# A new list of steps for chunk-selected attention and a gated MLP, planned with one reader at a time on a PSUM bank

## The chip, the cores and the metric

The kernel runs on one core of a Trainium2 chip. The metric is the device time of one execution, in microseconds, as the median of several runs. A profile is taken of one execution.

## The reference

Attention over 4 batches of 8 heads, 768 tokens, 64 columns a head, and then an MLP on the 3072 tokens of 512 columns.

```python
k_min, k_max = min and max of k over chunks of 32 keys
ub = sum(maximum(q * k_min, q * k_max), axis=-1)      # a bound per query and chunk
ub = where(causal, ub, -1e9)
sel = the 6 chunks with the largest ub, of each query
scores = where(sel & causal, q @ k.T / 8, -1e9)
attn = softmax(scores);  x = attn @ v                 # 8 heads side by side
h = x @ w_in                                          # 512 -> 2048
out = (h * clip(h + 3, 0, 6) / 6) @ w_out             # 2048 -> 512
```

## The kernel before

The work is cut into units and groups. A *unit* is half a batch of queries (384 tokens) for four heads, which are two *pairs* of heads; units u0 to u3 are batch 0, u4 to u7 batch 1, and so on, and pairs p0 to p3 are batch 0. In every batch the first two units are half 0, the other two half 1. A *group* is half a batch with all heads: g0 to g7.

For a pair and half the steps are: `turn` (TensorE transposes the keys, KS, or queries, QS, into a PSUM bank in batch 0; VectorE does it in later batches), `turn_out` (the queries' bank is copied to SBUF), `keys` (cast of the keys' bank), `limits` (two reductions on VectorE for minimum and maximum of each chunk, part 0, and a subtraction, part 1), `queries` (a relu, read from the bank in batch 0, and a cast). In batch 0 the keys' bank thus has two readers, `keys` and `limits`, and the queries' bank two, `turn_out` and the relu. Then, for a unit, `bounds` (TensorE), `bounds_in`, `bias`, `largest`, `select`, `guard`, `select_out` (VectorE, with POOL for some): the choice of chunks, which ends in a mask that `masks_out` copies beside the queries in batches 1 to 3. For a pair again: `scores` (TensorE, in two or four tiles), `exponentials` (ScalarE), `triangle` (POOL cuts the diagonal blocks), `values` (TensorE) and `values_out` (VectorE). `beside` and `shifted` copy constant mask rows next to keys.

For a group: `turn_tokens` (TensorE) or, for three groups, `turn_words`, a round trip through DRAM and `part_words`; `hidden` 0 to 15 (TensorE), `hidden_relu` and `hidden_out`; `result` (four parts of four matmuls per tile of 128 tokens, TensorE), `result_scale`, and a store on SP. The names with what they work on, as scores(p0 0 0) or hidden(g0 0), are used below.

K, Q and V are loaded by SP in an order written out in `SEQ` (line 661), four weight loads (two halves of w_in, WIN, and two of w_out, WOUT) are issued by POOL. Each weight load first reads a word of the input load that stands before it, so POOL waits there for that landing.

The order is planned while the program is built. `Plan.add` collects some 1,645 steps with the engines that can do them, what they come after, and which buffers they take and give (`m=4` PSUM banks for mixed use, `s=2` double banks for scores, and others). `Plan.order` (lines 74 to 132) runs through time with estimated lengths: whenever an engine is free it starts the ready step of the lowest rank for which there is room, and the steps are issued to the engines in that sequence. A rank comes from the list `PLACES` (line 978): the number of each listed step, in order. `ONLY` (line 1021) says which of the steps that several engines could do is done by which. Not listed are the loads and stores and 24 dummy matmuls (`busy`, line 339), which have the highest ranks and fill TensorE before the first inputs are there. `LANDED` (line 699) tells the planner when input loads land. On the chip the engines run their queues in the issued order and wait for each other by semaphores.

The readers of a bank in `prepare` (lines 801 to 824) and the list are what the change touches:

```python
turned[name] = seen[name] if name == "KS" else add(dict(ACT=0.45, DVE=0.52), None, r + lead, later(turn_out, st, name, half),
                                                   after=[seen[name]], take=[held[f]], give=[m])
...
for place, i in enumerate(PLACES.split()):
    plan.steps[int(i)]["rank"] = place, int(i)
```

Of the kernel before, what the change touches and what calls it, by code (L numbers as in the profile page):

```python
# [140 lines left out]
def kernel(  # L141
# [523 lines left out]
    plan = Plan(m=4, s=2, kf=4, qf=6, qr=6, ub=3, mt=2, pt=10, x=2, xt=2, bt=2, bd=2, gt=2, u=3, ot=2, vt=3, ks=2, qs=2, sel0=1, sel1=1, lane=8)  # L665
# [6 lines left out]
    def later(f, *args):  # L672
        return lambda *engine: f(*args, *engine)
# [6 lines left out]
    def arrive(engine, issue, length, run, after=(), take=(), parts=1):  # L680
# [3 lines left out]
        for part in range(parts):  # L684
# [14 lines left out]
    LANDED = dict(SP=[7.05, 7.65, 8.27, 8.87, 9.46, 10.07, 10.67, 11.26, 11.87, 12.47, 13.08, 13.68, 14.28, 14.88, 15.48, 16.08, 16.68, 17.28, 17.95, 19.70, 20.10, 20.50, 21.00, 21.40, 21.80, 22.35, 22.95, 23.55, 24.10, 25.10,  # L699
                      26.80, 41.00, 49.90, 51.40, 52.90, 54.20, 55.70, 57.20, 58.60, 60.00, 61.40, 62.80, 64.10, 64.80, 67.20, 68.80, 69.50, 70.40, 71.40, 72.20, 73.00, 73.70],  # L700
                  POOL=[33.30, 38.70, 44.50, 50.40])
# [379 lines left out]
```

## Time and profile before

| | |
|---|---|
| median of 3 runs | 266.26 us (266.20 to 266.56) |
| the profiled execution | 266.23 us |
| its span, first to last instruction | 264.4 us |
| TensorE (PE) busy | 258.8 us, 98% |
| VectorE (DVE) | 211.4 us, 80% |
| ScalarE (ACT) | 193.0 us, 73% |
| GpSimd (POOL) | 122.7 us, 46% |
| granted TensorE clock | full in all of 40 slices |

The span is counted from the first instruction; the execution's time also holds what lies around it. Line numbers (L350) are those of the kernel before. Matmuls are pipelined and their ends are modelled, so a busy TensorE can hide a wait. The chain is followed back from the last instruction: at each step to what released it.

### The profile page before, as it was taken

The page shows a single profiled execution, that of the slowest core. Times are in us where ns is not written, and L with a number is a line of the kernel's source. Part 1 is how long each engine was busy: PE and PEld are TensorE (multiplying, and loading weights), DVE is VectorE, ACT ScalarE, POOL GpSimd, SP SyncE. Part 2 cuts the span into 40 slices and gives each one's busy share as a digit, 9 for nine tenths or more (in the row PEclk, how much of TensorE's full clock was granted, in tenths as well). Part 3 has the DMA queues.
Part 4 walks back from the last instruction along what each step waited for, and adds up shares of the span by engine and source line. Part 5 has one row for each costly group of instructions (what it writes and reads, how often), then busy time and mean ns, then how long its engine had stood idle before and what let it go on. Part 6 is the DMA issues. An engine that isn't in the chain of part 4 may idle for free.

```text
span 264.4 us, 6698 instructions
## 1 busy us (share of the span) xinstructions
PE 258.8 (98%) x2468; PEld 153.8 (58%) x2468; DVE 211.4 (80%) x587; ACT 193.0 (73%) x318; POOL 122.7 (46%) x286
## 2 busy tenths in 40 slices
PE   8999999999999999999999999999999999999995
PEld 4547657655545666655655576654666575645543
DVE  6698987999979899997979799999997056905920
ACT  5869798597866999994986699965988686703601
POOL 8355624265545764465174793776464241020000
PEclk9999999999999999999999999999999999999999
DMA  8999999999949999951981999423000411132012
GB/s 165 219 211 174 209 198 217 167 133 159 233 117 135 145 199 134 138 134 42 151 70 45 216 166 136 99 102 116 26 0 4 159 42 41 62 99 79 2 40 79
DMA packets 121280, 32.15 MB, mean 122 GB/s; under 512 B 113056, under 2 KB 116896, under 8 KB 121248
## 3 DMA queue, kind: packets, MB, share of 16 engines
q1 hardware_dynamic: 116512, 27.14, 61.9%
q0 software_dynamic: 3136, 4.19, 9.3%
q10 hardware_dynamic: 1600, 0.39, 0.7%
q8 instruction: 19, 0.31, 0.5%
q14 instruction: 13, 0.11, 0.2%
HBM read 28.44 MB, written 7.47 MB: 136 GB/s over the span
## 4 chain that ended last, share of the span: by engine, by line
PE 87%; ACT 6%; DVE 2%; DMA 2%; issue 1%; ACTq 1%; DVEq 0%
PE HP L607 30%; PE OP L625 30%; PE SPS L517 10%; PE PVP L550 7%; ACT PT L529 4%; PE UBT L435 4%; DMA QS<-in_q_dram 2%; PE SPS L498 1%; PE OP L634 1%; PE XTP L571 1%; PE SPS L501 1%; ACTq L198 1%; PE SPS L342 1%; DVE KMA L374 1%; DVE KMA L375 1%
## 5 line engine op out<-in xcount | busy, mean ns | idle before, releaser
L529 ACT ACTIVATE PT<-SPS 128x1024 bf16<-128x1024 f32 (+2 forms) x96 | 84.8, 922 | 12.4 <-PE SPS L517 5.7
L607 PE MATMUL HP<-XT,WIN 128*128 128x384 bf16 x512 | 90.0, 326 | 0.0
L625 PE MATMUL OP<-WOUT,GT 128*128 128x512 bf16 x368 | 85.6, 379 | 0.0
L615 ACT ACTIVATE U<-HP,THREE 128x384 bf16<-128x384 f32 x100 | 57.4, 584 | 18.5 <-PE HP L607 14.6
L618 DVE SCALAR_TENSOR_TENSOR GT<-U,HP 128x384 bf16<-128x384 bf16 x128 | 66.2, 544 | 4.7 <-ACT U L615 2.4
L607 PEld LDWEIGHTS <-WIN 128*128 128x128 bf16 x512 | 48.5, 98 | 32.2 <-issue 1.9
L625 PEld LDWEIGHTS <-GT 128*128 128x128 bf16 x368 | 35.0, 98 | 37.2 <-issue 1.1
L534 POOL TENSOR_SCALAR_AFFINE_SELECT PT<-PT 128x256 bf16<-128x256 bf16 x84 | 33.9, 413 | 45.9 <-ACT PT L529 44.8
L517 PE MATMUL SPS<-QLA,KL 128*128 128x384 bf16 (+2 forms) x240 | 35.9, 278 | 0.5 <-ACT PT L529 0.4
L517 PEld LDWEIGHTS <-KL 128*128 128x128 bf16 x240 | 21.6, 98 | 12.9 <-issue 1.5
L651 ACT ACTIVATE OT<-OP 128x512 f32<-128x512 f32 x17 | 10.2, 597 | 24.6 <-PE OP L625 24.1
L550 PEld LDWEIGHTS <-PT 128*128 128x128 bf16 x672 | 24.3, 97 | 4.3 <-DVE Xb L562 0.3
L550 PE MATMUL PVP<-VB,PT 128*128 128x65 bf16 x672 | 25.9, 193 | 0.0
L309 POOL TENSOR_SCALAR_AFFINE_SELECT KL<-KF 64x384 bf16<-64x384 f32 x37 | 18.4, 501 | 8.2 <-DVE KF L359 7.1
L309 POOL TENSOR_SCALAR_AFFINE_SELECT QLA<-QF 64x384 bf16<-64x384 f32 (+1 forms) x32 | 16.0, 502 | 10.6 <-DVE QF L359 3.6
L562 DVE TENSOR_TENSOR Xb<-PVP,RINV 128x384 bf16<-128x384 f32 x32 | 18.2, 570 | 1.1
L613 DVE TENSOR_SCALAR U<-HP 128x384 bf16<-128x384 f32 x28 | 15.3, 547 | 3.5 <-PE HP L607 3.4
L556 DVE RECIPROCAL RINV<-PVP 128x6 f32<-128x6 f32 x32 | 5.9, 185 | 12.3 <-PE PVP L550 12.1
L392 ACT ACTIVATE QR<-QF 128x192 bf16<-128x192 f32 (+2 forms) x36 | 13.2, 413 | 1.7 <-DVE QF L359 1.6
L653 DVE TENSOR_SCALAR OT<-OP 128x512 f32<-128x512 f32 x6 | 4.1, 684 | 12.6 <-PE OP L625 12.6
L374 DVE TENSOR_REDUCE KMA<-KF 128x12 f32<-128x384 f32 x24 | 13.0, 540 | 0.3
L600 POOL COPY XT<-BF 128x384 bf16<-128x384 bf16 x12 | 5.6, 505 | 16.4 <-DMA BF<-BD 16.4
(92 smaller groups left out, 309.3 us busy)
## 6 DMA issues: line engine op xcount, KB each, us to landing
out_dram<-OT SPq DMA_DIRECT2D x23, 256.0 KB, 2.3
KS<-in_k_dram SPq DMA_DIRECT2D x24, 192.0 KB, 5.5
QS<-in_q_dram SPq DMA_DIRECT2D x24, 192.0 KB, 5.8
VT<-in_v_dram SPq DMA_DIRECT2D x24, 192.0 KB, 4.6
WIN<-in_moe_w_in_dram POOLq DMA_DIRECT2D x2, 1024.0 KB, 10.9
WOUT<-in_moe_w_out_dram POOLq DMA_DIRECT2D x2, 1024.0 KB, 19.4
VS<-in_v_dram SPq DMA_DIRECT2D x12, 128.0 KB, 3.7
KS<-in_k_dram SPq DMA_DIRECT2D x9, 128.0 KB, 3.9
```

What stands on the lines that cost most here:

```text
L309: nc.gpsimd.affine_select(out=to, in_=x, pattern=[[0, n]], compare_op=A.is_ge, fill=0.0, base=0, channel_multiplier=0)
L374: nc.vector.tensor_reduce(out=over, in_=chunks, axis=X_AXIS, op=A.max)
L517: nc.tensor.matmul(SP[:, j, c0:c0 + n], lhsT=KLS[st["pair"] % 6][:, j, jb * P:(jb + 1) * P], rhs=st["QL", half][:, j, at:at + n], start=Tr ...
L529: nc.scalar.activation(PT[:, :, 0:cols], SP[:, :, 0:cols], ACT.Exp, scale=scale)
L534: nc.gpsimd.affine_select(out=PT[:, :, c0:c0 + P], in_=PT[:, :, c0:c0 + P], pattern=[[0, 2], [1, P]], compare_op=A.is_ge, fill=0.0, base=0 ...
L550: nc.tensor.matmul(PVP[:, j, n, :], lhsT=PT[:, j, c0:c0 + P], rhs=st["VB"][:, jb, j, :], start=(jb == 0), stop=(jb == qb))
L562: nc.vector.tensor_tensor(out=to, in0=PVP[:, :, :, 0:D], in1=RINV[:].to_broadcast([P, 2, HB, D]), op=A.mult)
L607: nc.tensor.matmul(HP[:], lhsT=WIN[:, kt, f * P:(f + 1) * P], rhs=g["XT"][:, kt, :, :], start=(kt == 0), stop=(kt == KT_HID - 1))
L613: nc.vector.tensor_scalar(U[:], g["HP", f][:], 3.0, 0.0, op0=A.add, op1=A.max)
L615: nc.scalar.activation(U[:], g["HP", f][:], ACT.Relu, bias=THREE[:], scale=1.0)
L618: nc.vector.scalar_tensor_tensor(out=g["GT"][:, f, :], in0=g["U", f][:], scalar=6.0, in1=g["HP", f][:], op0=A.min, op1=A.mult)
L625: nc.tensor.matmul(g["OP", t][:], lhsT=g["GT"][:, f, t * P:(t + 1) * P], rhs=WOUT[:, f, :], start=(f == 0), stop=(f == FT - 1))
```

## The change

Three things change. The planner gets 16 new holds, `r0` to `r15`, one for each turned bank of batch 0 (keys or queries, pair, half), each with room for one; every reader of a bank takes the hold of its bank and gives it back, so the planner lets one engine at a time read it. The planner's landing times are replaced by new ones. And the list has new places for its 1,329 steps: 150 of the steps that several engines can do are given to another engine.

```diff
-    plan = Plan(m=4, s=2, ..., lane=8)
+    plan = Plan(m=4, s=2, ..., lane=8, **{f"r{i}": 1 for i in range(2 * H)})
...
-    LANDED = dict(SP=[7.05, 7.65, 8.27, 8.87, 9.46, 10.07, 10.67, 11.26, 11.87, 12.47, 13.08, 13.68, 14.28, 14.88, 15.48, 16.08, 16.68, 17.28, 17.95, 19.70, 20.10, 20.50, 21.00, 21.40, 21.80, 22.35, 22.95, 23.55, 24.10, 25.10,
-                      26.80, 41.00, 49.90, 51.40, ...],
-                  POOL=[33.30, 38.70, 44.50, 50.40])
+    LANDED = dict(SP=[7.05, 7.65, 8.25, 8.84, 9.45, 10.04, 10.64, 11.24, 11.85, 12.47, 13.06, 13.66, 14.26, 14.86, 15.47, 16.07, 16.66, 17.27, 17.84, 19.43, 19.91, 20.33, 20.72, 21.05, 21.57, 22.10, 23.01, 23.59, 24.07, 25.11,
+                      27.59, 41.46, 50.28, 51.20, ...],
+                  POOL=[32.30, 38.62, 44.06, 49.91])
...
+            def alone(name):
+                return [hold(f"r{4 * p + 2 * half + (name == 'QS')}")] if first else []
...
+                    one = alone(name)
                     turned[name] = seen[name] if name == "KS" else add(dict(ACT=0.45, DVE=0.52), None, r + lead, later(turn_out, st, name, half),
-                                                                       after=[seen[name]], take=[held[f]], give=[m])
+                                                                       after=[seen[name]], take=[held[f]] + one, give=[m] + one)
...
+            one = alone("KS")
             made["K", p, half] = [add(dict(DVE=0.52, ACT=0.51) if first else castings(first), None, r + lead + 1, later(keys, st, half, j), port=not first,
-                                      after=[a] + free.get(("KL", p - 6), []), give=read) for j in range(1 if first else 2)]
-            b1 = add("DVE", 1.0 if first else 0.93, r + lead, later(limits, st, half, 0), after=[a] + free.get(("KM", p - 6), []), give=read)
+                                      after=[a] + free.get(("KL", p - 6), []), take=one, give=read + one) for j in range(1 if first else 2)]
+            one = alone("KS")
+            b1 = add("DVE", 1.0 if first else 0.93, r + lead, later(limits, st, half, 0), after=[a] + free.get(("KM", p - 6), []), take=one, give=read + one)
...
-                             after=[seen["QS"] if first else c], take=[u["qr", p]], give=banks.get("QS", [u["qf", p]]), port=not first)]
+                             after=[seen["QS"] if first else c], take=[u["qr", p]] + one, give=banks.get("QS", [u["qf", p]]) + one, port=not first)]
...
     PLACES = """
-        156 337 153 335 160 144 164 147 146 152 155 157 159 168 331 145 165 161 167 169 158 162 170 163 166 181 154 171 333 172 185 184 182 186 190
...
+        156 154 331 152 335 333 146 159 164 147 153 145 337 144 157 160 155 167 165 158 161 168 170 163 162 169 166 173 181 171 177 172 184 176 178
+        174 185 182 175 183 190 180 231 179 186 191 187 239 188 192 236 189 244 193 232 194 240 237 238 195 245 230 210 241 196 200 234 207 211 197
...
```

The steps that the prediction speaks of, with their places in the queue of their engine as the two lists give them:

| number | step | before | after |
|---|---|---|---|
| 152, 153 | shifted(0), shifted(1) | POOL 5, 1 | DVE 1, 3 |
| 333 | beside(1 1) | ACT 10 | DVE 2 |
| 159, 160 | keys(p0 0 0), limits(p0 0 0) | ACT 4, DVE 1 | ACT 3, DVE 4 |
| 167, 168 | keys(p1 0 0), limits(p1 0 0) | DVE 3, DVE 2 | ACT 5, DVE 5 |
| 177, 185 | limits(p2 0 0), limits(p3 0 0) | DVE 9, 6 | DVE 7, 9 |
| 190, 192, 195 | bounds_in(u0), largest(u0), select_out(u0) | DVE 7, 10, 14 | DVE 10, 11, 14 |
| 172 | bounds(u0) | PE 6 | PE 7 |
| 207 | cast_values(p1 0) | POOL 17 | ACT 21 |
| 197, 217 | exponentials(p0 0 0), exponentials(p2 0 0) | ACT 20, 26 | ACT 22, 28 |
| 313 | cast_values(p2 1) | POOL 23 | ACT 37 |
| 90 | second weight load, WIN | POOL 27 | POOL 24 |
| 273, 276, 279 | triangle(p0 1 1), (p0 1 2), (p0 1 3) | POOL 32, 31, 33 | POOL 29, 30, 32 |
| 330 | beside(0 0) | DVE 38 | POOL 31 |
| 281, 1028 | values(p0 1), hidden(g0 0) | PE 41, 44 | PE 41, 44 |
| 295 | values(p1 1) | PE 56 | PE 47 |
| 332 | beside(1 0) | ACT 41 | DVE 43 |
| 482, 491, 492 | queries(p6 1 0), (p7 1 0), (p7 1 1) | ACT 103, ACT 106, POOL 85 | POOL 82, POOL 87, ACT 110 |
| 1367 | hidden_out(g4 15) | DVE 279 | DVE 281 |
| 952 | limits(p15 1 0) | DVE 273 | DVE 295 |
| 864, 957 | bounds(u12,u13), bounds(u14,u15) | PE 265, 272 | PE 263, 270 |
| 1405 | hidden(g5 0) | PE 273 | PE 275 |

On TensorE 153 of its 386 listed steps keep their place, and the last 50 or so differ by one or two swaps.

## Rows read from the trace of the kernel before

**Rows 1.** The page's first part: busy us, share of the span, instructions.
```profile
PE 258.8 (98%) x2468; PEld 153.8 (58%) x2468; DVE 211.4 (80%) x587; ACT 193.0 (73%) x318; POOL 122.7 (46%) x286
```

**Rows 2.** Busy time by stage: length, engines with instructions, clock, DMA share, GB/s.
```profile
4.02:20.42 16.40, 15.63 (x150) 8.94 (x149) 13.12 (x48) 12.74 (x25) 7.92 (x22) 1.00 1.26 213
...
95.00:261.40 166.40, 166.40 (x1507) 99.34 (x1503) 127.28 (x336) 119.14 (x197) 71.51 (x164) 1.00 0.51 90
261.40:264.40 3.00, 0.01 (x1) 0.00 (x0) 0.29 (x1) 0.00 (x0) 0.00 (x0) 1.00 0.25 87
```

**Rows 3.** The chain that ended last, in order: start, length, what.
```profile
8.87 1.42 PE UBT L435 x16
...
37.82 1.03 ACT PT L529
...
89.64 1.63 ACT PT L529 x2
...
170.94 1.73 PE OP L625 x8
...
183.26 1.45 PE UBT L435 x32
...
240.61 10.40 PE HP L607 x64
```

**Rows 4.** Who waited for whom, 4 to 20 us: total, times, longest.
```profile
ACT KL L305 <- DVE KMA L375: 1.1, 2, 0.8
...
DVE KMA L374 <- ACT KL L305: 0.9, 1, 0.9
...
DVE QR L394 <- ACT QF L224: 0.5, 1, 0.5
```

**Rows 5.** The tile WIN, 0 to 40 us: issue (ns, starts) and landing.
```profile
L293 POOL DMA_DIRECT2D WIN<-in_moe_w_in_dram x2: 791/891/991, 23.2 to 26.0; - x2
...
DMA to landing us min/median/max: 9.1/10.9/12.6
```

**Rows 6.** Timeline of VectorE, 4.9 to 18 us: start, length, what, idle before.
```profile
4.98 0.56 DVE L374 TENSOR_REDUCE KMA<-KT 128x12 f32<-128x384 f32 x1 [0.86 <-PE KT L350]
...
12.62 0.56 DVE L374 TENSOR_REDUCE KMA<-KT 128x12 f32<-128x384 f32 x1 [0.93 <-ACT KL L305]
...
14.92 0.56 DVE L470 STREAM_TRANSPOSE MT<-SELA 128x384 bf16<-128x384 bf16 x1
```

**Rows 7.** Line 226 to 50 us: copies of mask rows on VectorE, ns least/median/most.
```profile
L226 DVE COPY KL<-EB x4: 353/539/708, 29.5 to 46.8; 64x768 bf16<-64x768 bf16 x4
```

**Rows 8.** Timeline of ScalarE, 14 to 38 us: exponentials(p0 0 0) and exponentials(p2 0 0).
```profile
16.16 1.02 ACT L529 ACTIVATE PT<-SPS 128x1024 bf16<-128x1024 f32 x1 [1.61 <-PE SPS L505]
...
21.19 1.02 ACT L529 ACTIVATE PT<-SPS 128x1024 bf16<-128x1024 f32 x1 [0.17 <-PE SPS L505]
```

**Rows 9.** Timeline, 28.2 to 33.6 us: values(p0 1) and hidden(g0 0) on TensorE.
```profile
31.27 1.09 PE L550 MATMUL PVP<-VB,PT 128*128 128x65 bf16 x30
...
33.16 0.66 PE L607 MATMUL HP<-XT,WIN 128*128 128x384 bf16 x3
```

**Rows 10.** Timeline of POOL, 20 to 33 us: weight loads, last triangle of p0.
```profile
25.86 0.17 POOL L290 COPY seenWIN<-VS 1x1 f32<-1x1 f32 x1
...
28.13 0.87 POOL L296 DMA_DIRECT2D WOUT<-in_moe_w_out_dram  x1
...
30.74 0.41 POOL L534 TENSOR_SCALAR_AFFINE_SELECT PT<-PT 128x256 bf16<-128x256 bf16 x1 [0.96 <-ACT PT L529]
```

**Rows 11.** Timeline, 86 to 95 us: TensorE's longest wait there.
```profile
91.63 0.60 PE L517 MATMUL SPS<-QLA,KL 128*128 128x256 bf16 x4 [0.43 <-ACT PT L529]
```

**Rows 12.** Timeline of VectorE, 167 to 185 us: limits(p15 1 0), hidden_out(g4 15), bounds_in(u13).
```profile
169.91 0.54 DVE L374 TENSOR_REDUCE KMA<-KF 128x12 f32<-128x384 f32 x1
...
173.17 0.52 DVE L618 SCALAR_TENSOR_TENSOR GT<-U,HP 128x384 bf16<-128x384 bf16 x1
...
178.16 0.58 DVE L439 STREAM_TRANSPOSE UB<-UBT 128x384 f32<-128x384 f32 x1 [0.19 <-PE UBT L435]
```

More of the change, by code (lines that the diff above doesn't have):

```diff
@@ L664 @@
         [RANK[f"{k}{i}"] for i in range(m)] for k, m in (("l", 16), ("t", 16), ("s", 16), ("v", 16), ("b", 16), ("g", 8), ("h", 8), ("o", 8), ("a", 8)))
-    plan = Plan(m=4, s=2, kf=4, qf=6, qr=6, ub=3, mt=2, pt=10, x=2, xt=2, bt=2, bd=2, gt=2, u=3, ot=2, vt=3, ks=2, qs=2, sel0=1, sel1=1, lane=8)
+    plan = Plan(m=4, s=2, kf=4, qf=6, qr=6, ub=3, mt=2, pt=10, x=2, xt=2, bt=2, bd=2, gt=2, u=3, ot=2, vt=3, ks=2, qs=2, sel0=1, sel1=1, lane=8, **{f"r{i}": 1 for i in range(2 * H)})
     plan.room["gt"].remove(1)
@@ L697, in arrive @@
         return landed
-    LANDED = dict(SP=[7.05, 7.65, 8.27, 8.87, 9.46, 10.07, 10.67, 11.26, 11.87, 12.47, 13.08, 13.68, 14.28, 14.88, 15.48, 16.08, 16.68, 17.28, 17.95, 19.70, 20.10, 20.50, 21.00, 21.40, 21.80, 22.35, 22.95, 23.55, 24.10, 25.10,
-                      26.80, 41.00, 49.90, 51.40, 52.90, 54.20, 55.70, 57.20, 58.60, 60.00, 61.40, 62.80, 64.10, 64.80, 67.20, 68.80, 69.50, 70.40, 71.40, 72.20, 73.00, 73.70],
-                  POOL=[33.30, 38.70, 44.50, 50.40])
+    LANDED = dict(SP=[7.05, 7.65, 8.25, 8.84, 9.45, 10.04, 10.64, 11.24, 11.85, 12.47, 13.06, 13.66, 14.26, 14.86, 15.47, 16.07, 16.66, 17.27, 17.84, 19.43, 19.91, 20.33, 20.72, 21.05, 21.57, 22.10, 23.01, 23.59, 24.07, 25.11,
+                      27.59, 41.46, 50.28, 51.20, 52.80, 54.00, 55.80, 57.00, 58.50, 59.90, 61.40, 62.80, 64.20, 64.90, 67.20, 68.80, 69.50, 70.40, 71.40, 72.20, 73.00, 73.70],
+                  POOL=[32.30, 38.62, 44.06, 49.91])
     FIRST = dict(KS=(3.65, 4.63), QS=(5.6, 6.43))
@@ L822, in prepare @@
             u["qr", p], u["qf", p] = hold("qr"), held["qf"]
+            one = alone("QS")
             chain += [c, add(dict(ACT=0.44, DVE=0.5) if first else dict(ACT=0.55 if coarse(st["b"], half) else 0.42), None, r + lead, later(queries, st, half, "relu"),
-                             after=[seen["QS"] if first else c], take=[u["qr", p]], give=banks.get("QS", [u["qf", p]]), port=not first)]
+                             after=[seen["QS"] if first else c], take=[u["qr", p]] + one, give=banks.get("QS", [u["qf", p]]) + one, port=not first)]
             made["Q", p, half] = [add(castings(first), None, r + lead + 1, later(queries, st, half, j), port=True,
@@ L978 @@
     PLACES = """
[41 rows of a table removed]
-        1609 1607 1614 1612 1610 1617 1613 1620 1615 1618 1616 1623 1621 1619 1622 1624 1630 1625 1626 1631 1627 1632 1633 1637 1634 1641 1638 1642"""
[41 rows of a table added]
+        1617 1615 1613 1620 1616 1623 1618 1621 1619 1624 1622 1625 1630 1631 1626 1632 1627 1633 1637 1634 1641 1638 1642"""
     ONLY = {
         "ACT": """
[6 rows of a table removed]
-            1591 1597 1600 1603 1609 1612 1618 1621 1634 1638""",
[6 rows of a table added]
+            1612 1615 1621 1627 1638""",
         "DVE": """
-            162 163 167 175 178 214 235 240 243 250 254 258 262 280 330 334 336 338 383 384 406 409 411 499 628 800 869 871 963 1025 1027 1029 1035
-            1041 1050 1053 1059 1065 1094 1153 1171 1173 1178 1187 1190 1205 1211 1233 1246 1248 1287 1317 1324 1327 1330 1339 1421 1436 1445 1464
-            1491 1509 1549 1576 1579 1594 1606 1615 1627 1642""",
+            152 153 169 184 214 235 240 243 249 250 280 300 332 333 381 409 497 499 622 656 741 744 798 997 1025 1027 1029 1041 1044 1047 1053 1062
+            1065 1098 1153 1167 1171 1173 1178 1184 1190 1193 1202 1208 1214 1220 1251 1260 1269 1275 1306 1319 1321 1327 1333 1336 1342 1354 1406
+            1409 1412 1418 1421 1445 1471 1491 1497 1500 1509 1518 1521 1536 1542 1594 1609 1618 1634 1642""",
         "POOL": """
[3 rows of a table removed]
-            932 933 937 941 946 947 950 951 956 961 964 994 996 997""",
[3 rows of a table added]
+            947 950 951 955 956 961 963 994 996""",
     }
```

97 rows, old and new, of tables (ONLY, PLACES) are left out of this document.

## The prediction

> **What bounds the kernel now.** I read the busy shares first, then a table by stage, the chain of work that ended last, the waits, and the timelines of single engines. TensorE is busy for 258.8 of 264.4 us [rows 1]. The stage table says where the rest is: from 95.00 to 261.40 us it is busy for 166.40 of 166.40, and 3.00 us follow its last matmul [rows 2]. The change adds and removes no matmul, so in that stretch a new order can gain next to nothing, and can lose. Before 95 us there is something to gain: at 37.82 and at 89.64 the chain runs through ScalarE's exponentials, which TensorE waits for [rows 3], and from 4 to 20 us it is mostly VectorE's and ScalarE's. In that first stretch the busy share of TensorE [rows 2] hides waits: dummy matmuls fill it, and ends of matmuls are modelled. The granted clock is 1.00 in the stages shown [rows 2], so nothing is to be had from it.
>
> Why the first stretch is slow is in the waits between readers of one bank: the cast of the keys waits for the bounds' reductions (1.1 us in two waits), a reduction for the cast (0.9), and a relu for a copy of the queries (0.5) [rows 4]. The kernel before thus already has one engine at a time on a bank; only its list does not know it.
>
> **The holds and the landings** issue no instruction and no wait. They change what the planner thinks, and with it the list. I cost them at nothing; the waits of [rows 4] already exist. The new landings are those of this trace: the first half of WIN is issued at 23.2 and lands 9.1 us later [rows 5], at 32.3, and the diff writes 32.30. The order of the input loads on SP is not touched. On POOL the four weight issues keep their order; the second is three places earlier.
>
> **The list up to the first hidden matmul.** TensorE's own order up to hidden(g0 0) differs by a few places, so what matters is when its inputs come. I walk the new queues with durations from rows.
> VectorE was free 0.86 us before 4.98 [rows 6]. It now copies three mask rows (152, 333, 153) first. Four such copies took 0.353 to 0.708 us [rows 7], so these take 1.1 to 2.1 us, to 5.2 to 6.2; and the first reduction must now let ScalarE cast the keys first, at some 5.8. So limits(p0) starts 0.9 to 1.3 us later than the 4.98 of before, and limits(p1) ends near 8.2. That slip is covered: the next keys are turned only at about 8.4, when they have landed (the diff's 8.25). If that cover is gone, up to 0.3 us passes on to bounds(u0).
> From there the new order gains. Before, the reduction at 12.62 waited 0.93 for the cast of the same bank, with the choice of chunks (192) queued behind it, and the mask was turned at 14.92 [rows 6]. Now both reductions (177, 185) stand ahead of 190, and the choice follows at once. From bounds(u0) at 9.05 to 10.45 (1.42 us as in [rows 3]): VectorE's reductions to 11.35, bounds_in to 11.9, bias and choice to 13.4, the copy of a query bank to 13.9, and the mask's turn starts there, 1.0 us earlier.
> But ScalarE now casts values (207) ahead of the first exponential, and the diff has them land at 15.47. So that exponential starts at about 15.95, against 16.16 [rows 8]: 0.2 us. Later ones gain more, as two bank waits are gone: exponentials(p2 0 0) at some 20.25 against 21.19 [rows 8].
> Then most is given back on POOL. values(p0 1) at 31.27 [rows 9] needs the triangle cut at 30.74 [rows 10]. POOL's weight issues now end at about 28.85 against 29.00, since its second issue, ready at 25.86 before [rows 10], comes half a microsecond earlier and one value cast has gone to ScalarE. Yet a mask copy (330, up to 0.8 us) now stands between the triangles (276, 279). That gives the last triangle at 30.45 to 30.85, values(p0 1) at 30.85, and hidden(g0 0) at 32.7 against 33.16 [rows 9]. It can't start before 32.3, when WIN lands [rows 5]. So this part gains 0.45, between 0 (the mask copy holds the triangle to 31.2) and 0.86 (33.16 less 32.3).
>
> **33 to 95 us.** At 37.82 scores(p2 1 3) waited for an exponential [rows 3], some 0.29 us. In the new list values(p1 1), 0.92 us of work, comes ahead of those scores, and a mask copy of 0.8 us (332) has left ScalarE: exponentials(p1 1 3) comes about 1.2 us earlier, and the wait goes. Gain 0.29, between 0 and 0.3. The wait at 89.64 stays: between the exponentials of half 0 and half 1 ScalarE loses queries(p7 1 0) and gets queries(p7 1 1), both casts of 0.5 us; the cast taken away before (482) stood in an idle gap. TensorE's wait of 0.43 at 91.63 [rows 11], and the two smaller ones beside it, stay: 0, at best 0.5.
>
> **95 us to the end.** Between turn_tokens_out(g2 0) and bounds_in(u8) I count 53 VectorE steps in either list, so I see no new wait there. Farther on the new list gives VectorE more relus (29 come from ScalarE, 16 go to it, over the whole kernel). One move stands out: limits(p15 1 0), at 169.91 before [rows 12], goes from place 273 to 295 of VectorE's queue. It now stands behind the choice of u12, and bounds(u14,u15) needs it; that one stood in the chain at 183.26 [rows 3] and now goes out two result steps (0.86 us each, as eight such matmuls took 1.73 [rows 3]) earlier, so TensorE would reach it at about 181.5 on the old clock. Thirteen VectorE items lie between hidden_out(g4 15), 173.17 before [rows 12], and the end of limits(p15 1 0). By durations as in [rows 12] (0.56 a reduction, 0.52 a product, overlapped by a tenth) they take 8.2 us. If VectorE reaches hidden_out(g4 15) when it did and is free at 173.6, that step and its POOL subtraction of 0.2 end at 182.0, and TensorE waits 0.5. But from values_out(p10 0) to hidden_out(g4 15) the new list has one VectorE step less, 0.6 us, and TensorE lets the first go 0.2 earlier: then it ends at 181.2, and TensorE waits nothing. I take 0.2, nearer to the second; the ends are 0 and 0.9, a step of limits more. The round trip of group 5 through memory starts four places later on VectorE (turn_words(g5 1)), and hidden(g5 0), which reads it, goes out two places later on TensorE: 0. On SP the stores go where their result tiles go; none stands in the chain. The last two steps of TensorE are the same: 0.
>
> **Sum.** The profiled execution took 266.23 us, 0.03 less than the median of 266.26, and 1.83 more than its span. 266.23 - 0.45 - 0.29 - 0 + 0.2 = 265.69, so 265.7.
>
> **A rule that says more is to be had.** The 64 hidden matmuls from 240.61 take 10.40 us [rows 3], 0.1625 us each, and [rows 2] leaves no gap: I take the late stretch as full. The Trainium skill (Trainium Kernel Development and Optimization, Performance Expectations) calls matmul busy time a bad metric, as matmuls are pipelined, and looks at the share of weight loads instead. That share is 58% here [rows 1]. By it the late stretch would not be full and order could gain there too. The 0.1625 us speak against it.
>
> **Rivals.** First, *more gain*: the early part wins its whole 0.86, the wait near 90 us loses 0.5, and bounds(u14,u15) waits for nothing: 266.23 - 0.86 - 0.29 - 0.5 = 264.6. For it: two bank waits of [rows 4] fall away. Against: WIN's landing and POOL's queue stand behind. A late stretch that is not full would end up here as well, at 265 or less.
> Second, *slower*, by the step on VectorE: with its relus VectorE comes 1.5 us late to limits(p15 1 0), TensorE waits behind bounds(u14,u15) with the scores of batch 3 queued after it, and nothing later makes that good, since TensorE is full to the end. 266.23 - 0.74 + 1.5 = 267.0. It decides from the point at which that reduction ends after 181.3 on the old clock; every microsecond beyond is lost. For it: VectorE's one pause in the stretch shown, at 178.16, was 0.19 us [rows 12]. Against: the count of steps.
> Third, *nothing moves*: POOL's mask copy gives the early gain back, and the 0.29 is spent at bounds(u14,u15): 266.2. That the holds do nothing is part of it: they only tell the planner what the semaphores enforce [rows 4].
>
> **How the numbers follow.** A measurement of this kernel tells 0.2%, 0.53 us, from no change, so faster means below 265.7. The forecast case (265.3 to 266.0) has 0.45; its middle lies on that bound, and I give 0.27 of it to faster. More gain has 0.18, nothing moves 0.15, slower 0.22, of which 0.02 stay within the bound. That makes faster 0.45, same 0.35, slower 0.20. The range goes from 264.6, more gain, to 267.0, slower; beyond its ends lies some 0.15.
>
> **What would show it.** Right: no wait of a reduction for a cast of the same bank, the first mask's turn near 13.9, the first exponential at 15.9 to 16.2, values(p0 1) near 30.9, hidden(g0 0) near 32.7, and the wait at 91.6 unchanged. Wrong: hidden(g0 0) at 33.2 or later; a wait of TensorE for VectorE's KMA or POOL's subtraction near 181; any new wait of TensorE after 95 us.

## The result: 1.2% slower, and the profile after

The changed kernel takes 269.41 us (median of 4 runs, 269.39 to 269.52) against 266.23 us of the kernel before beside it (266.15 to 266.56): a ratio of 1.0119, interval 1.0104 to 1.0134. The prediction said 265.7 with a range of 264.6 to 267.0. It is wrong in sign and size: even its *slower* rival ended at 267.0. The profiled execution took 269.43 us, its span is 267.7 us.

The page of the changed kernel, its first part, which answers to [rows 1]:

```profile
span 267.7 us, 6693 instructions
PE 259.7 (97%) x2468; PEld 152.7 (57%) x2468; DVE 215.8 (81%) x595; ACT 190.6 (71%) x315; POOL 121.6 (45%) x281
```

The span grew by 3.3 us and TensorE's busy time by 0.9: some 2.4 us are gaps in TensorE. The table by stage finds most of them. Columns: stretch, its length, busy time of TensorE (matmuls), of its weight loads, of VectorE, ScalarE and POOL, granted clock, share and rate of the DMA engines. The kernel before:

```profile
84.00:97.00 13.00, 12.47 (x152) 8.59 (x151) 11.51 (x35) 12.65 (x18) 10.08 (x24) 1.00 1.26 162
```

The same view of the changed kernel, and the rest of it:

```profile
84.00:97.00 13.00, 10.62 (x115) 6.89 (x114) 10.18 (x44) 11.41 (x15) 10.39 (x22) 1.00 0.96 144
97.00:264.00 167.00, 166.98 (x1512) 99.35 (x1511) 133.92 (x351) 115.84 (x191) 69.16 (x159) 1.00 0.51 91
```

TensorE idles 2.38 us from 84 to 97 us, before 0.53. From 97 us on it is as full as it was [rows 2], so whatever is lost before stays lost. The chain of the changed kernel from 80 to 97 us shows for what it idles:

```profile
81.36 1.45 PE UBT L435 x32
82.81 1.83 PE OP L625 x8
84.64 0.45 PE SPS L517 x4
...
85.17 1.03 ACT PT L529
...
88.95 1.51 ACT PT L529 x2
90.49 0.83 ACT QLA L224
91.32 3.22 ACT PT L529 x4
```

This is the first use of batch 1: the scores of its first unit (SPS), then its exponentials (PT) on ScalarE one after another, and little result work (OP) between. In the kernel before the same scores went out 3.5 us earlier, and TensorE had a longer stock of result matmuls to do beside the exponentials. On TensorE a few steps date the slip. Starts in us, from the timelines of TensorE; e1 to e10 are experiments below, and the last column is free of the start-up, which varies from run to run by over 1 us. Each row is one trace; a second trace of the changed kernel (e5) has 231.51 in the last column for 231.30:

| kernel | hidden(g0 0) | bounds(u4,u5) | scores(p4 0 0) | first hidden matmul to last matmul |
|---|---|---|---|---|
| before | 33.16 | 73.29 | 80.96 | 228.25 |
| after | 33.47 | 76.79 | 84.48 | 231.30 |
| e1, list kept | 33.10 | 72.85 | 80.53 | 229.21 |
| e2, no third result | 34.22 | 74.08 | 81.76 | 229.94 |
| e3, third result put back | 33.83 | 76.17 | 83.86 | 230.95 |
| e6, and loads ahead | 34.43 | 74.18 | 81.86 | 228.75 |
| e7, and triangle first | 33.22 | 72.97 | 80.65 | 228.75 |
| e10, old landings | 33.70 | 73.56 | 81.24 | 228.78 |

Of the 3.36 us by which the last matmul ends later (264.77 against 261.41), 0.31 arise ahead of hidden(g0 0) and 3.05 behind it. bounds(u4,u5) comes 3.50 later, 3.20 of it behind hidden(g0 0).

### The profile page after: what moved, and what is told of

The parts are those of the page before. It is cut to its first block, busy times and chain, and to the rows that moved or that the text cites. A ratio compares the mean times of both kernels' runs of the same rounds, so it can differ in the third digit from the quotient of the medians.

```text
span 267.7 us, 6693 instructions
## 1 busy us (share of the span) xinstructions
PE 259.7 (97%) x2468; PEld 152.7 (57%) x2468; DVE 215.8 (81%) x595; ACT 190.6 (71%) x315; POOL 121.6 (45%) x281
## 4 chain that ended last, share of the span: by engine, by line
PE 83%; ACT 5%; SPq 3%; POOL 3%; DMA 3%; issue 2%; DVE 0%; POOLq 0%; ACTq 0%
PE HP L607 31%; PE OP L625 30%; PE SPS L517 9%; PE PVP L550 7%; ACT PT L529 4%; PE UBT L435 3%; SPq L200 2%; DMA VS<-in_v_dram 1%; PE OP L634 1%; DMA KS<-in_k_dram 1%; PE SPS L498 1%; SPq L214 1%; PE SPS L501 1%; PE XTP L571 1%; POOL WIN L293 1%
## 5 line engine op out<-in xcount | busy, mean ns | idle before, releaser
L607 PE MATMUL HP<-XT,WIN 128*128 128x384 bf16 x512 | 91.8, 326 | 0.0
L529 ACT ACTIVATE PT<-SPS 128x1024 bf16<-128x1024 f32 (+2 forms) x96 | 83.8, 921 | 11.3 <-PE SPS L517 7.7
L618 DVE SCALAR_TENSOR_TENSOR GT<-U,HP 128x384 bf16<-128x384 bf16 x128 | 67.0, 546 | 13.4 <-ACT U L615 10.9
L615 ACT ACTIVATE U<-HP,THREE 128x384 bf16<-128x384 f32 x87 | 49.5, 584 | 15.0 <-PE HP L607 12.5
L613 DVE TENSOR_SCALAR U<-HP 128x384 bf16<-128x384 f32 x41 | 22.4, 547 | 7.1 <-PE HP L607 7.0
L309 POOL TENSOR_SCALAR_AFFINE_SELECT QLA<-QF 64x384 bf16<-64x384 f32 (+1 forms) x37 | 18.8, 510 | 10.2 <-PE SPS L517 3.1
L309 POOL TENSOR_SCALAR_AFFINE_SELECT KL<-KF 64x384 bf16<-64x384 f32 x32 | 16.0, 501 | 6.9 <-DVE KF L359 5.9
L374 DVE TENSOR_REDUCE KMA<-KF 128x12 f32<-128x384 f32 x24 | 13.0, 543 | 0.4
L359 DVE STREAM_TRANSPOSE KF<-KS 128x384 f32<-128x384 f32 x24 | 13.3, 562 | 0.0
L375 DVE TENSOR_REDUCE KMA<-KF 128x12 f32<-128x384 f32 x24 | 13.0, 543 | 0.0
L359 DVE STREAM_TRANSPOSE QF<-QS 128x384 f32<-128x384 f32 x24 | 12.5, 550 | 0.0
## 6 DMA issues: line engine op xcount, KB each, us to landing
WIN<-in_moe_w_in_dram POOLq DMA_DIRECT2D x2, 1024.0 KB, 10.9
```

What stands on the lines that cost most here:

```text
L309: nc.gpsimd.affine_select(out=to, in_=x, pattern=[[0, n]], compare_op=A.is_ge, fill=0.0, base=0, channel_multiplier=0)
L359: nc.vector.transpose(T[:], st[name][:, st["i"], half * HC:(half + 1) * HC, :].rearrange("p c e -> p (c e)"))
L529: nc.scalar.activation(PT[:, :, 0:cols], SP[:, :, 0:cols], ACT.Exp, scale=scale)
L607: nc.tensor.matmul(HP[:], lhsT=WIN[:, kt, f * P:(f + 1) * P], rhs=g["XT"][:, kt, :, :], start=(kt == 0), stop=(kt == KT_HID - 1))
L613: nc.vector.tensor_scalar(U[:], g["HP", f][:], 3.0, 0.0, op0=A.add, op1=A.max)
L615: nc.scalar.activation(U[:], g["HP", f][:], ACT.Relu, bias=THREE[:], scale=1.0)
```

## Where the queue leaves the list

The prediction walked the list as if it were the queue. TensorE's timeline of the changed kernel shows it is not (columns: start, length, engine, line, operation and tiles, count):

```profile
54.87 2.11 PE L607 MATMUL HP<-XT,WIN 128*128 128x384 bf16 x12
56.82 1.03 PE L625 MATMUL OP<-WOUT,GT 128*128 128x512 bf16 x4
57.68 2.11 PE L607 MATMUL HP<-XT,WIN 128*128 128x384 bf16 x12
59.63 1.03 PE L625 MATMUL OP<-WOUT,GT 128*128 128x512 bf16 x4
```

After three hidden steps comes a result step at 56.82. In the list hidden(g1 3) has place 282 and result(g0 1 0) place 298. The planner (`Plan.order`) took the higher place first: it runs through time, and a free engine takes the lowest-ranked step that is ready *at that moment*. By its clock hidden(g1 2) ends on TensorE at 56.66050632911391 and a step on POOL at 56.6605063291139. The two are the same moment but for rounding; POOL's event is handled first, TensorE counts as free (`free[e] > now + 1e-9` is false), yet hidden(g1 3), which becomes ready with hidden(g1 2)'s own event, is not in the list of ready steps. So result(g0 1 0) goes out. It is the first of nine places on TensorE where a step goes out ahead of one that stands before it in the list. In the kernel before the issued order equals the list on every engine, which is why I had taken one for the other.

What that does is seen some 15 us later. TensorE's timeline of the kernel before:

```profile
70.82 2.54 PE L625 MATMUL OP<-WOUT,GT 128*128 128x512 bf16 x11
73.29 0.28 PE L435 MATMUL UBT<-QLA,KMA 64*32 64x192 bf16 x8
```

and of the changed kernel:

```profile
71.73 5.13 PE L625 MATMUL OP<-WOUT,GT 128*128 128x512 bf16 x23
76.79 0.28 PE L435 MATMUL UBT<-QLA,KMA 64*32 64x192 bf16 x8
```

The planner has four mixed banks (`m=4`). result(g,t) takes one with its part 0 and gives it back only when `result_scale`, after part 3, has read it. As the hidden steps come later, hidden_out(g1 14) can be used on TensorE 0.18 us too late for result(g1 1 0), at planner time 72.37, while result(g1 0 0), which needs 12 of the 16 hidden_out and stands far down the list, is ready and is taken. Then three results are open (g0 2, g1 0 and g1 1), one bank is left, and bounds(u4,u5) needs two: it waits for result_scale(g0 2). A second tie adds to that: this bank comes back at 75.825 by the planner's clock, the moment at which TensorE is free, but for rounding, so result(g1 1 3), 0.865 us long, still goes out first. TensorE is not idle meanwhile, it does result work. But that work was to cover the exponentials of batch 1, and from 84 to 97 us it is missing.

## The experiments

**e1, the list kept.** Events of one moment are taken in together, so that a tie can't put a step out of the list.

```diff
+            if events and events[0][0] <= now + 1e-9:
+                continue
             for e, steps in ready.items():
```

> The changed kernel, with one alteration in its planner: engines choose their next step only after all events of the same moment (to within rounding) have been taken in. With it every engine issues its steps in the order of the list as written. Theory 'wrong turn' (the changed kernel is slow since its planner leaves the list at hidden(g1 3), where result(g0 1 0) goes out first): TensorE's waits between 84 and 95 us go back to about 1 us, bounds(u4,u5) at 73.3 and not 76.8, and the time is 265.4 to 266.5. Rival 'the list itself' (too many relus on VectorE, exponentials late for whatever order): 268.5 to 269.5, with bounds(u4,u5) still after 75.

Measured: 267.90 us, ratio 1.0042 (1.0024 to 1.0059). Lines are numbered two higher here. The timeline of TensorE has the seven hidden steps together:

```profile
54.50 4.80 PE L609 MATMUL HP<-XT,WIN 128*128 128x384 bf16 x28
...
72.85 0.28 PE L437 MATMUL UBT<-QLA,KMA 64*32 64x192 bf16 x8
```

Behind hidden(g0 0) 2.09 of the 3.05 us come back (231.30 to 229.21), and bounds(u4,u5) comes even 0.44 earlier than before. The tie is the larger cause. The time itself lies between what the two theories said, 1.4 us above the first and 0.6 below the second. 0.96 remain, and from the gain of 0.37 up to bounds(u4,u5) they must all be lost later. VectorE's timeline of e1 names the place (in brackets the idle time ahead of it and what ended it):

```profile
115.90 1.04 DVE L361 STREAM_TRANSPOSE QF<-QS 128x384 f32<-128x384 f32 x2 [0.94 <-DMA QS<-in_q_dram]
```

and the chain of e1 runs through the load that it waits for:

```profile
109.13 6.30 DMA QS<-in_q_dram
```

A load of queries is late, and TensorE then waits 0.35 us for VectorE at turn_tokens(g3). SP's queue of e1 shows what stands ahead of the loads:

```profile
77.27 6.52 SPq L659 DMA_DIRECT2D out_dram<-OT  x2
83.84 5.20 SPq L210 DMA_DIRECT2D KS<-in_k_dram  x4
```

Before, the same four loads of keys were issued from 80.69:

```profile
77.06 3.53 SPq L657 DMA_DIRECT2D out_dram<-OT  x2
80.69 3.75 SPq L208 DMA_DIRECT2D KS<-in_k_dram  x4
```

One of the stores in front of them, result_out(g1 2), waits for its result, and the loads wait behind it. In the changed kernel itself the loads start at 86.05, but everything there is 3 us late, and VectorE waits for no load of queries: this loss is hidden under the first one.

**e2 and e3, the order and the bank apart.** e2 is the changed kernel, overtakings and all, with result(g1 0 0) held back until bounds(u4,u5) is out. e3 is e1 with result(g1 0 0) put in the list just ahead of result(g1 1 0), so that the third result is opened on purpose; nothing overtakes ahead of it, but steps that lack a bank are overtaken behind it.

```diff
 e2:
-                            after=prev + gts[:max(12, 4 * part + 4) if t == 0 else FT] + there["WOUT", part // 2],
+                            after=prev + gts[:max(12, 4 * part + 4) if t == 0 else FT] + there["WOUT", part // 2]
+                                  + ([made_units[4]["bounds"]] if (b, half, t, part) == (0, 1, 0, 0) else []),
 e3, in the list of e1:
-... 375 374 1156 467 ... 495 482 1149 390 ...
+... 375 374 1149 1156 467 ... 495 482 390 ...
```

> The changed kernel as it is, wrong turn at hidden(g1 3) kept, but result(g1 0 0) may go out only after bounds(u4,u5). Theory 'bank' (the loss comes from the third open result, result(g1 0), which holds one of four PSUM banks, so that bounds(u4,u5), which needs two, waits): bounds(u4,u5) at 73.5 to 74.0, no waits for exponentials at 86 to 94, 266.0 to 267.0. Rival 'filler spent' (four result steps pulled ahead among the hidden steps of group 1 are missing as cover later): 268.5 or more, with the waits at 86 to 94 as they were. Rival 'late hidden steps': also 268.5 or more, with bounds(u4,u5) late.

> The list kept as in the first run of this call, with a single step moved in it: result(g1 0 0) stands just ahead of result(g1 1 0), so that three results are open when bounds(u4,u5) comes up. No step is pulled ahead of hidden(g1 3). Theory 'bank': bounds(u4,u5) moves from 73.3 to about 75.5, scores(p4 0 0) to 83 or later, and the time is 268.0 to 269.3, nearly the whole loss. Rival 'filler spent': one step of 0.86 us taken ahead costs 0 to 0.4 us, 265.4 to 266.5.

Measured: e2 267.25 us, ratio 1.0031 (1.0010 to 1.0053); e3 269.52 us, ratio 1.0092 (1.0067 to 1.0118). Both lie some 0.2 above what the theory of the bank said, and 1.2 and 3.0 from its rivals. Counted from hidden(g0 0), bounds(u4,u5) comes at 39.86 in e2 (74.08 less 34.22) and at 39.75 in e1: the overtaken hidden steps by themselves move it 0.11. In e3 it comes at 42.34, 2.59 later than in e1, and the gap from 84 to 97 us is there again. TensorE's timeline and the table by stage of e3:

```profile
70.68 5.56 PE L627 MATMUL OP<-WOUT,GT 128*128 128x512 bf16 x25
76.17 0.28 PE L437 MATMUL UBT<-QLA,KMA 64*32 64x192 bf16 x8
```

```profile
84.00:97.00 13.00, 10.98 (x121) 7.21 (x119) 10.43 (x44) 11.50 (x15) 9.81 (x23) 1.00 0.81 132
```

So the bank is the mechanism, and the tie only what set it off. It makes up 1.74 of the 2.09 (230.95 less 229.21). In e3 bounds(u4,u5) comes 0.98 less late than in the changed kernel, about the 0.865 of the second tie and the 0.11 of the hidden steps. e2 still loses 0.73 more than e1 behind hidden(g0 0): there TensorE waits 1.0 at turn_tokens for VectorE, which waits 1.6 for the late queries.

**e4, the slip alone in the kernel before.** hidden(g1 3) is made to wait, in the planner, for result(g0 1 0).

```diff
-            before = [add("PE", 0.65, ..., later(hidden, g, f), after=xt + before + there["WIN", f * 2 // FT],
+            before = [add("PE", 0.65, ..., later(hidden, g, f), after=xt + before + there["WIN", f * 2 // FT] + (slipped if (b, half, f) == (0, 1, 3) else []),
...
+                if (b, half, t, part) == (0, 0, 1, 0):
+                    slipped = prev[:]
```

> The kernel before, with the wrong turn forced on it: hidden(g1 3) waits for result(g0 1 0) in the planner. In its list no third result is opened ahead of bounds(u4,u5). Theory 'bank': the wrong turn alone costs little, 0.3 to 1.0 us, so 266.5 to 267.3. Rival 'filler spent' or 'late hidden steps': about the loss of the changed kernel, 268.7 to 269.7.

Measured: 267.48 us, ratio 1.0025 (1.0010 to 1.0040). The time is 0.2 above the range. From hidden(g0 0), bounds(u4,u5) is 0.62 later (40.74 for 40.12), the last matmul 0.64. The bank isn't opened here, and TensorE is busy for 12.47 of the 13 us from 84 to 97, as before: the slip alone costs a quarter of a per cent, not 1.2%.

**e5, the changed kernel again**, unaltered, on the chip of e6 to e8.

> The changed kernel once more, unaltered, so that it stands beside its variants on one chip. All theories: 269.0 to 270.2, as in the result.

Measured: 269.66 us, ratio 1.0123 (1.0105 to 1.0141). The loss repeats.

**e6, the loads ahead of the store.** e1, with result_out(g1 2) placed behind the loads of keys of pairs 8 and 9.

```diff
+            issued[name, n] = issued["SP"][-1]
...
-            a = add("SP", 0.37, -2000, later(result_out, g, t, nc.sync), after=[a], take=[lane])
+            a = add("SP", 0.37, -2000, later(result_out, g, t, nc.sync), after=[a] + ([issued["KS", 8]] if (b, half, t) == (0, 1, 2) else []), take=[lane])
```

> The list kept (as in the run e1), and on SP the store of the tile result_out(g1 2) put behind the four key loads of pairs 8 and 9 in place of ahead of them. Theory 'store ahead of the loads' (in e1 that store waits on SP for its result until 83.4, so the load stream of batch 2's second half and of batch 3 starts 3 us later than before, at 83.84 against 80.69, the last query load lands at 115.4, VectorE waits for it 0.9, and TensorE 1.0 at 117 and 122): the loads start at 80.5 to 81.5, no wait for a query load at 115, and 0.8 to 1.3 us less than e1: 266.2 to 267.2 on this chip. Rival 'relus on VectorE' (VectorE is late by itself, the load only shares the blame): TensorE's waits at 117 and 122 stay, 267.4 to 268.4.

Measured: 266.96 us, ratio 1.0020 (1.0007 to 1.0033). SP's queue:

```profile
76.07 2.88 SPq L659 DMA_DIRECT2D out_dram<-OT  x2
79.05 3.61 SPq L210 DMA_DIRECT2D KS<-in_k_dram  x4
```

The wait for the queries is gone, and 0.46 more come back (229.21 to 228.75). The intervals of e1 and e6 overlap, and the planner, which reckons with the earlier loads, also moves a few steps on other engines: on TensorE result(g2 1 3) now stands ahead of turn_tokens(g3), where e1 waits, and may have covered a part of it.

Three runs price the late loads better, since from bounds(u4,u5) on they issue the same queues: e1, e2 and e10 (the changed kernel with the old landings, below), with loads from 83.84, 85.07 and 84.55. Ahead of the turn of the queries near 116 us VectorE stands still for 0.94 us in e1, 1.58 in e2 and 0.42 in e10, where it waits for no load. Its waits from 94 to 126 us in e2 and in e10:

```profile
DVE QF L359 <- DMA QS<-in_q_dram: 1.6, 1, 1.6
```

```profile
DVE QF L359 <- issue: 0.4, 1, 0.4
```

From the first hidden matmul to the last they take 229.21, 229.94 and 228.78: 0.73 more in e2 than in e1 for 0.64 more of this pause, 0.43 less in e10 for 0.52 less. With the same queues it is the landing that differs: the load took 6.30 us in e1, 6.93 in e2, and at most 5.3 in e10, issued at 110.8 and used at 116.08. So a late stream costs what the landing makes of it in one execution: next to nothing in the trace of e10 (228.78, against 228.75 of e6 with early loads), and 0.46 in that of e1. The profiled executions took 266.98 (e1, the least of its 12 runs), 268.83 (e2, the most) and 267.14 (e10, below its median).

**e8, the loads behind a store in the kernel before.** The loads of keys of pairs 8 and 9 are put behind result_out(g0 2).

```diff
+            n_issued = len(issued["SP"])
...
+            issued[name, n] = issued["SP"][n_issued]
...
+            if (b, half, t) == (0, 0, 2):
+                a["then"].append(issued["KS", 8])
+                issued["KS", 8]["wait"]["SP"] += 1
```

> The kernel before, with the key loads of pairs 8 and 9 put behind the store result_out(g0 2) on SP, so that the stream starts at about 88.2 and not at 80.69. Theory 'store ahead of the loads': the last query load of pairs 10 and 11 lands at 116 to 120 where VectorE wants it at 115.9, VectorE and then TensorE wait: 267.3 to 271. Rival 'the loads are hidden anyway': 266.2 to 266.8.

Measured: 268.10 us, ratio 1.0059 (1.0045 to 1.0074). SP's queue, and then the waits of VectorE from 94 to 126 us (in total, times, longest):

```profile
77.01 11.20 SPq L657 DMA_DIRECT2D out_dram<-OT  x3
88.26 2.41 SPq L208 DMA_DIRECT2D KS<-in_k_dram  x3
```

```profile
DVE RINV L556 <- PE PVP L550: 2.0, 1, 2.0
DVE QF L359 <- DMA QS<-in_q_dram: 0.6, 1, 0.6
```

With loads 7.57 us later the kernel before loses 1.42 us behind hidden(g0 0) (229.67 for 228.25). The planner reckons with them here too and moves steps on all engines: values_out(p4 1) now stands ahead of the turns of the late keys on VectorE, and the 2.0 is its wait for TensorE. The wait for a load itself is 0.6. So e8 shows what late loads cost together with the order that the planner makes of them, and not the wait alone.

**e7, the triangle first.** e6, with the mask copy beside(0 0) placed behind the last triangle that values(p0 1) needs.

```diff
+                        issued["tri", p, half] = parts[-1]
...
-                made["EB", i] = [add(..., later(beside, i, j), after=free["KL", i if i < 4 else -1] if j == 0 or i == 5 else [],
+                made["EB", i] = [add(..., later(beside, i, j), after=(free["KL", i if i < 4 else -1] if j == 0 or i == 5 else []) + ([issued["tri", 1, 1]] if (i, j) == (0, 0) else []),
```

> As e6, and on POOL the mask copy beside(0 0) behind triangle(p1 1 3 256) in place of between the triangles of pair 0. Every other engine keeps its order. Theory 'POOL gates values(p0 1)': its last triangle comes some 0.6 us earlier, the wait inside values(p0 1) (0.46 in the changed kernel, 0.13 in e1) goes, hidden(g0 0) starts at 32.5 to 33.1: 0.1 to 0.4 us less than e6. Rival 'WIN bounds it': hidden(g0 0) starts when the first half of WIN lands, 32.7 to 33.8 in the runs so far, so 0 to 0.1.

Measured: 266.65 us, ratio 1.0007 (0.9994 to 1.0020): no longer to be told from the kernel before. Behind hidden(g0 0) e7 takes the same 228.75 as e6. The 0.31 between their medians lies ahead of it, and their intervals overlap; in the two traces WIN landed at 33.1 (e7) and 34.4 (e6), with hidden(g0 0) at 33.22 and 34.43. POOL's timeline of the changed kernel shows the cost, and how late the weight issues end:

```profile
25.96 0.17 POOL L290 COPY seenWIN<-VS 1x1 f32<-1x1 f32 x1 [0.63 <-DMA VS<-in_v_dram]
...
28.73 0.88 POOL L296 DMA_DIRECT2D WOUT<-in_moe_w_out_dram  x1
29.62 0.79 POOL L534 TENSOR_SCALAR_AFFINE_SELECT PT<-PT 128x256 bf16<-128x256 bf16 x2
30.47 0.82 POOL L228 TENSOR_SCALAR_AFFINE_SELECT KL<-EB 64x768 bf16<-64x768 bf16 x1
31.36 0.41 POOL L534 TENSOR_SCALAR_AFFINE_SELECT PT<-PT 128x256 bf16<-128x256 bf16 x1
```

The mask copy of 0.82 us puts the last triangle at 31.36, against 30.74 [rows 10]. In e7 that triangle is ready for POOL and waits for something else:

```profile
30.80 0.41 POOL L536 TENSOR_SCALAR_AFFINE_SELECT PT<-PT 128x256 bf16<-128x256 bf16 x1 [1.12 <-ACT PT L531]
```

The brackets give the idle time ahead of it: 1.12 us for ScalarE's exponential. POOL bounded this point in the changed kernel; ScalarE bounds it at 30.80 when POOL is out of the way, no earlier than the 30.74 of before. There was no gain over the kernel before to be had from POOL here.

**e10 and e11, the landings and the holds apart.** e10 is the changed kernel with the old `LANDED`. e11 is e7 without the holds (`alone` returns an empty list).

```diff
 e11:
-                return [hold(f"r{4 * p + 2 * half + (name == 'QS')}")] if first else []
+                return []
```

> The changed kernel with its list and holds, but with the old landings in the planner: only constants of the planner's clock differ, no instruction's work. The planner still leaves the list at hidden(g1 3), but comes back to it: result(g1 0 0) goes out after bounds(u4,u5). Theory 'bank': the time is that of the run e2, 266.5 to 267.9, 2 us less than the changed kernel. Rival 'filler spent' or 'the list itself': 269 to 270.

> As e7, but without the holds of the turned keys' and queries' banks: the planner may again give two engines one bank at a time, and nine pairs of neighbours before 35 us change places (limits(p0 1 0) and limits(p1 1 0) on VectorE, keys(p0 1 0) and exponentials(p0 0 0) on ScalarE, among them). Theory 'the holds only say what the semaphores do': within 0.3 us of e7, 266.3 to 267.0 on this chip. Rival 'the holds save bank waits': 0.4 to 0.9 us more than e7, with reductions and casts of one bank waiting for each other at 15 to 17 us.

Measured: e10 268.04 us, 0.14 above the range of its theory, ratio 1.0047 (1.0025 to 1.0069); e11 266.78 us, ratio 1.0010 (0.9998 to 1.0021), against 1.0007 of e7. The holds are worth nothing that can be measured. The landing times, which issue no instruction, are worth some 0.7%: with the old ones the hidden steps are still overtaken, but result(g1 0 0) is not opened early, bounds(u4,u5) comes 39.86 behind hidden(g0 0), as in e2, and the last matmul 228.78 behind it. The loads start late there too, at 84.55, without a wait for them in this trace, as said at e6.

**e9 and e12, the one gain of the prediction that came, put into the kernel before.** At 37.82 TensorE waited for an exponential [rows 3]; the new list has values(p1 1) earlier. e9 moves that step (295) alone ahead of hidden(g0 3) in the list (the planner issues it right behind). e12 moves with it the next scores and exponentials (302, 304, 303, 305), and takes the mask copy beside(1 0) (332) from ScalarE to VectorE.

```diff
 e9:
-... 293 1030 1037 1033 ... 309 1049 295 1047 ...
+... 293 1030 295 1037 1033 ... 309 1049 1047 ...
 e12:
-... 293 1030 1037 1033 302 1035 1038 1036 304 303 1039 1040 305 1043 ... 1049 295 1047 ...
+... 293 1030 295 302 304 303 305 1037 1033 1035 1038 1036 1039 1040 1043 ... 1049 1047 ...
     and 332 from "ACT" to "DVE" in ONLY
```

> The kernel before, with values(p1 1) moved in its list ahead of hidden(g0 3) and with what the planner makes of that: on TensorE and VectorE some steps between 35 and 48 us change places, all else keeps its order. Theory 'cover at 37.8' (the one gain of the new list that its traces show: the wait of 0.29 us of scores(p2 1 3) for an exponential goes): 0.2 to 0.35 us less, 265.9 to 266.3 where the kernel before has 266.2 to 266.5. Rival 'the exponential is late too' (the scores go out later as well, so the wait moves with them): 0 to 0.1.

> The kernel before with the part of the new list that its traces show to gain, and nothing else: ahead of hidden(g0 3) stand values(p1 1), scores(p2 1 0), scores(p2 1 1) and their exponentials, and the mask copy beside(1 0) goes from ScalarE to VectorE. Theory 'ScalarE's queue' (the wait of scores(p2 1 3) goes when the copy of 0.84 us, and the relu of hidden(g0 3), no longer stand ahead of the exponentials): no wait at scores(p2 1 3), 0.25 to 0.4 us less than the kernel before, 265.8 to 266.2. Rival 'the landing of WIN sets it' (hidden(g0 0) and all behind it move with a landing that differs by over 2 us from run to run): within 0.15 us, not to be told from no change.

Measured: e9 266.60 us, ratio 0.9999 (0.9987 to 1.0011); e12 266.23 us against 266.50 on its chip, ratio 0.9987 (0.9977 to 0.9998). In e9 the wait moved along: values(p1 1) ahead of the scores pushes them back, and with them the exponentials that later scores wait for (to 38.55, from 36.90 before, of which 0.75 is hidden(g0 0) at 33.91). ScalarE's timeline of e9:

```profile
38.55 1.94 ACT L529 ACTIVATE PT<-SPS 128x1024 bf16<-128x1024 f32 x2 [1.25 <-PE SPS L501]
```

In e12 the scores come early too and the mask copy of 0.83 is off ScalarE. Its two pairs of exponentials:

```profile
36.89 1.94 ACT L529 ACTIVATE PT<-SPS 128x1024 bf16<-128x1024 f32 x2 [1.59 <-PE SPS L501]
...
39.81 1.73 ACT L529 ACTIVATE PT<-SPS 128x768 bf16<-128x768 f32 x2
```

The second no longer has a bracket, so ScalarE waits for nothing there, and from 33.27 to 43.94 the chain of e12 runs through TensorE alone. From the first hidden matmul to the last one e12 takes 227.94 for 228.25: 0.31 us, about the wait of 0.29 that the prediction priced. That is one trace of each. By the times e12 is ahead of both kernels, though by an interval that only just excludes no change.

## Why the prediction was wrong, point by point

**The step that failed** is "The holds and the landings issue no instruction and no wait. They change what the planner thinks, and with it the list. I cost them at nothing". The list stands fixed in the kernel; what the planner thinks changes the *issued order* under it. The walk through the new queues was a walk through the list. e1 prices the difference at 2.09 us behind hidden(g0 0), e3 shows that the open bank carries 1.74 of it, and e10 that, with the hidden steps overtaken, the landings decide whether the bank is opened. I had quoted the rule of `Plan.order` (the lowest rank *for which there is room*, among the ready steps) and not asked where a step might not be ready.

**"On SP the stores go where their result tiles go; none stands in the chain"** failed as well. Going where the tiles go, one store came to stand ahead of four loads, and SP issued them only behind it. In the changed kernel itself no engine waits for that; where the first loss is gone it costs 0.46 us in the trace of e1 and next to nothing in that of e10.

**The early gain of 0.45** came out as a loss of 0.31: hidden(g0 0) at 33.47, predicted 32.7. The first half of the walk held on VectorE. The changed kernel's timeline:

```profile
4.13 1.84 DVE L226 COPY KL<-EB 32x768 bf16<-32x768 bf16 x3
6.06 0.56 DVE L374 TENSOR_REDUCE KMA<-KT 128x12 f32<-128x384 f32 x1
...
12.70 0.19 DVE L452 TENSOR_REDUCE T<-UB 128x6 f32<-128x36 f32 x1 [0.87 <-POOL UB L443]
...
14.06 0.57 DVE L470 STREAM_TRANSPOSE MT<-SELA 128x384 bf16<-128x384 bf16 x1
```

The three mask copies took 1.84 us (1.1 to 2.1 said), the first reduction starts at 6.06 (5.9 to 6.3 follows from it), the mask is turned at 14.06 (13.9 said, 14.92 before). The reduction's wait for the cast (0.9) and the relu's (0.5) of [rows 4] are gone, and a wait of 0.87 for POOL's bias is new. But the earlier mask moved no scores. TensorE's timeline of the kernel before:

```profile
15.39 0.34 PE L498 MATMUL SPS<-QLA,KL 64*128 64x384 bf16 x2
```

and of the changed kernel:

```profile
14.59 0.88 PE L350 MATMUL KT<-IDENT,KS 128*128 128x128 f32 x6
15.39 0.34 PE L498 MATMUL SPS<-QLA,KL 64*128 64x384 bf16 x2
```

scores(p0 0 0) starts at 15.39 in both. In the new queue the turns of the second half's keys of p1 and p0, six transposes, stand right ahead of it (before, that of p0 came behind), and TensorE shows no wait there. "TensorE's own order up to hidden(g0 0) differs by a few places, so what matters is when its inputs come" was the step that failed here: that order had not been walked. ScalarE's timeline of the changed kernel:

```profile
15.81 0.52 ACT L224 CAST VB<-VS 128x384 bf16<-128x384 f32 x1 [0.16 <-DMA VS<-in_v_dram]
16.23 1.02 ACT L529 ACTIVATE PT<-SPS 128x1024 bf16<-128x1024 f32 x1
...
21.14 1.02 ACT L529 ACTIVATE PT<-SPS 128x1024 bf16<-128x1024 f32 x1 [0.33 <-PE SPS L505]
```

The scores of the first exponential end at about 16.1 in both kernels, so it could not come at 15.95; the cast of values at 15.81 ahead of it costs only 0.07 (16.23 for 16.16). The one at 21.14 for a predicted 20.25 gained 0.05 on the 21.19 of before: its scores went out no more than that earlier (20.37 against 20.42). On POOL the second weight issue waited 0.63 for a landing of values, the issues ended at 29.61 (28.85 said), and the mask copy did the rest. The term's own lower end, "the mask copy holds the triangle to 31.2", was the right reading; it lay at 31.36, below the range.

**The 0.29 at 37.8** is right: in the changed kernel scores(p3 1 0) starts at 41.75, as before, though hidden(g0 0) was 0.31 late, and e12 gives the like. **The wait near 90 us** was to stay; in the changed kernel it is lost in the larger gap, and in e1, where that is gone, two waits stand in its place, 0.21 for an exponential and 0.27 for POOL's triangle. **The 0.2 at bounds(u14,u15)** was nothing: no wait stands there in the changed kernel. **The late stretch** is full, 166.98 of 167.00 us, as said; the rule of the Trainium skill that matmul busy time is a bad metric (Trainium Kernel Development and Optimization, Performance Expectations), from which the prediction drew that order could gain in this stretch too, is of no help here: a loss made before 97 us was not won back in it.

Taken off one after the other, from trace to trace, the 3.36 us are 0.31 ahead of hidden(g0 0), 2.09 by the overtakings and the bank, 0.46 by the late loads (with the moves of e6), and 0.50 that e6 and e7 still have against the kernel before. **Open** is that last half microsecond. e7 gains 0.37 up to bounds(u4,u5); some 0.5 of what it then loses lies between 92 and 122 us (reckoned with the planner's lengths of the steps between), where TensorE's longest wait is 0.22 for ScalarE at a result step, and no run isolates it. That a loss depends on a landing fits the scatter: the times of e1, e2 and e10, with late loads, spread over 1.8 to 2.5 us, those of e6, e7 and e11, with early ones, over 1.1 to 1.5. It is not shown to be the cause.

## What to carry to other kernels

A list of places handed to a scheduler is a priority, not an order: before pricing a new list, derive the order that is really issued, and check how near the ties are, since a changed estimate that issues nothing cost 0.7% here. An accumulation issued in parts holds its bank from the first part to the last, so a step pulled forward can starve one that needs two banks, and the busy engine hides this until its stock of cover is gone. On a queue that runs in order a store that waits for its result is a wait for every load behind it; and a large loss can hide a smaller one, so profile again once the first is mended.

## What the runs showed of the hardware that was not expected

The first half of WIN, one megabyte, landed 8.9 to 11.3 us after its issue from run to run (before 9.1, e12 8.9, e4 10.9, e6 11.3). In e3, e4, e5, e6 and e11 hidden(g0 0) waits for it, by 0.37 to 1.35 us. Over all runs it starts between 33.1 and 34.7 us, at 34.22 in e2 for a late POOL: 1.5 us of scatter in the start, enough to blur a comparison of spans, which counting from the first hidden matmul removes. And the issue of one 192 KB load of queries on SP lasts 0.3 to 2.3 us where loads follow one another (eight loads in the kernel before: 0.43, 1.21 and 1.69 as shortest, median and longest; e7 has the 0.31, e2 the 2.30), where the planner counts 0.6. Of a stream that starts 3.2 us later behind hidden(g0 0), in e1, 1.7 are left at its last load of queries (76.0 for 74.3).
